# A new step order for a fused attention and MLP kernel, with half of w_out scaled by ScalarE in 128-column steps

## The chip, the cores and the metric

The kernel runs on one core of a Trainium2 chip. A core has five engines with queues of their own: TensorE (PE, matrix products), VectorE (DVE), ScalarE (ACT), GpSimd (POOL) and SyncE (SP, which here only issues DMAs). The metric is device time in microseconds (us), lower is better. All times below come from three runs and one profiled execution of the kernel before.

## The reference, cut to what matters

Two parts, the second fed by the first. In the attention part every 32-element row x of q and k is turned into 64 features, all products of 8 + 8 projections; then kv and the normalisation are sums over 1088 positions, for 4 batches and 4 heads:

```python
phi(x) = outer(S1 @ x, S2 @ x).reshape(64)       # for each row of q and of k
kv  = einsum('bhsf,bhsd->bhfd', phi(k), v);  z = phi(k).sum(over s)
num = einsum('bhsf,bhfd->bhsd', phi(q), kv)
x   = num / (einsum('bhsf,bhf->bhs', phi(q), z)[..., None] + 1e-6)
```

The result, 4352 tokens of 128, goes through an MLP with 2048 hidden units:

```python
h = x @ w_in;  g = h * sigmoid(beta * h);  out = g @ w_out
```

## The kernel before, in words

**The MLP.** Column j of w_in is multiplied by beta (tile `winb`, f16) and row j of w_out by 1/beta (tile `woutp`, f16), so that the activation is a plain SiLU and needs no scale. w_in and w_out come and are scaled in four quarters of 512 columns or rows: steps `wb0` to `wb3` (line 340) and `wo0` to `wo3` (line 343). The tokens go in ten chunks (seven of 512, three of 256). A chunk's 16 blocks of hidden units are taken in "waves" of 1024 f32 PSUM columns, 68 waves in all. Step `f<n>a`/`f<n>b` (line 885) writes the two halves of wave n with x @ winb; with the second half ACT's SiLU (line 894, tile `gT`) is issued. Step `s<n>a`/`s<n>b` (lines 917 and 909) multiplies gT by woutp and adds into the chunk's accumulator. Wave tiles have two PSUM buffers, so PE can be at most two waves ahead of ACT. Quarter 0 of winb and woutp serves waves 0 and 1 of a chunk, quarter 1 waves 2 and 3, and so on. Steps `o<n>` store a chunk: a transpose on DVE, and DMAs on SP's queue.

**The attention,** once for each batch b: load k and q (`lk`, `lq`) and v (`lv`); turn k (`kta`, `ktb`, DVE), project (`kpj`, PE), turn back (`ktn`, DVE, tile `tk`), build the feature products in four pieces (`kp0` to `kp3`, POOL or DVE), and sum them with v on PE (`kv0` to `kv3`, line 610). For q the same (`qt`, `qpj`, `qtn`), with the denominators (`zs` to `dr`), scaled by the inverse (`an`), products (`qp`), turned (`qpt`, DVE). Then `num` (PE, line 708) gives the tokens and `xa`, `xb`, `xc` (ACT or DVE) copy them to `xall`, from which the waves read. Batch 0 goes another way, so that the first wave can start early: its first 512 tokens are done in a part of their own (`qt0x0`, `qpjx0`, `cpjx0`, `dpx0`, `numx0`), the denominators are spread by PE (`rxa0`, `rxb0`, line 564, tile `dr`), copied by ACT (`ry0`, line 574) and multiplied in by DVE (`xm00`, `xm10`, line 579). beta is spread to all partitions by PE for the first two quarters (`bp0`, `bp1`, line 317) and copied by ACT (`by0`, `by1`), and by DMA for the others (`lba2`, `lba3`). Small set-up steps stand first: `ls1`, `ls2`, `sp`, `sp2` for S1 and S2, `lb`, `lbb`, `bt`, `bc`, `rb` for beta.

**Idle matmuls.** A step `i<n>` issues n matmuls of zeros, 128x512 (line 373), whose result nobody reads; they only keep PE at work. Before has 16 of them.

**What sets the order.** There is no scheduler at run time. `ORDER` is a list of step names written out in full; the kernel runs through it and issues each step's instructions, so it fixes every engine's program order and the order of the DMAs on SP's queue. The engines run on their own, tied by semaphores. `ENGINES` says which engine does a step that could run on several ("p" POOL, "v" DVE, "a" ACT). A DMA on SP also waits until the eighth DMA before it has landed.

```python
    for name in ORDER.split():
        if name[0] == "i" and name[1:].isdigit():
            idle(int(name[1:]))
        else:
            ops.pop(name)()
```

## Time and profile before

| | |
|---|---|
| three runs | 103.53, 103.75 and 108.78 us, median 103.75 us |
| profiled execution | 103.81 us, of which the profile's span is 102.1 us |
| busy in the span | PE 96.1, ACT 74.9, DVE 59.8, POOL 50.9 us |
| first wave's first matmul | 19.28 us into the span |
| first SiLU | 19.92 us |
| last matmul's end | 98.5 us |

The table's last three lines are from the timeline of the profile. A busy PE is not PE at its peak: matmuls overlap, and a busy stretch can hold slow matmuls. Lines of the profile name an engine, the source line, the operation and the tiles, "out<-in". In the view of the chain, the work that ended last is followed backwards: each line has a start, a length and what ran then. "x4" counts instructions, "[2.01 <-PE wave L885]" says how long the engine had been idle before and what released it.

### The profile page before, as it was taken

The page shows a single profiled execution, that of the slowest core. Times are in us where ns is not written, and L with a number is a line of the kernel's source. Part 1 is how long each engine was busy: PE and PEld are TensorE (multiplying, and loading weights), DVE is VectorE, ACT ScalarE, POOL GpSimd, SP SyncE. Part 2 cuts the span into 40 slices and gives each one's busy share as a digit, 9 for nine tenths or more (in the row PEclk, how much of TensorE's full clock was granted, in tenths as well). Part 3 has the DMA queues.
Part 4 walks back from the last instruction along what each step waited for, and adds up shares of the span by engine and source line. Part 5 has one row for each costly group of instructions (what it writes and reads, how often), then busy time and mean ns, then how long its engine had stood idle before and what let it go on. Part 6 is the DMA issues. An engine that isn't in the chain of part 4 may idle for free.

```text
span 102.1 us, 3119 instructions
## 1 busy us (share of the span) xinstructions
PE 96.1 (94%) x1308; PEld 49.7 (49%) x1308; DVE 59.8 (59%) x109; ACT 74.9 (73%) x96; POOL 50.9 (50%) x60
## 2 busy tenths in 40 slices
PE   5999998999999999999999999999999999999960
PEld 1353468335444545353445454434444435689950
DVE  1256696799895795589996469698635020111110
ACT  1411526296798597478999669999968999999940
POOL 6503999498799997038997419539300000000000
PEclk9999999999999999999999999999999999999999
DMA  2999995789218628615620050123012214014221
GB/s 40 349 258 334 359 307 172 223 272 290 87 38 288 113 51 234 197 24 87 182 75 13 13 95 5 39 50 53 0 23 37 50 25 77 0 29 78 47 58 51
DMA packets 23998, 12.05 MB, mean 118 GB/s; under 512 B 17008, under 2 KB 21936, under 8 KB 23984
## 3 DMA queue, kind: packets, MB, share of 16 engines
q1 hardware_dynamic: 23744, 11.77, 43.6%
q8 instruction: 10, 0.16, 0.7%
q10 hardware_dynamic: 240, 0.08, 0.3%
q14 instruction: 4, 0.03, 0.2%
HBM read 9.32 MB, written 2.23 MB: 113 GB/s over the span
## 4 chain that ended last, share of the span: by engine, by line
PE 82%; ACT 10%; DVE 3%; issue 1%; ACTq 0%
PE wave L885 27%; PE acc L917 20%; ACT gT L894 9%; PE idle L373 5%; PE xp L708 5%; PE at L610 4%; PE fin L909 4%; PE kpp L390 3%; PE qpp L471 3%; PE kvb L610 1%; PE xw L708 1%; PE bw L317 1%; PE at L491 1%; PE at L434 1%; PE dr L564 1%
## 5 line engine op out<-in xcount | busy, mean ns | idle before, releaser
L894 ACT ACTIVATE gT<-wave 128x1024 f16<-128x1024 f32 (+1 forms) x69 | 65.3, 1017 | 8.0 <-PE wave L885 7.2
L885 PE MATMUL wave<-xall,winb 128*128 128x512 f16 (+1 forms) x128 | 36.2, 366 | 0.3
L917 PE MATMUL acc<-gT,woutp 128*128 128x512 f16 (+1 forms) x128 | 34.4, 365 | 0.0
L885 PEld LDWEIGHTS <-winb 128*128 128x128 f16 x160 | 14.8, 98 | 16.0 <-issue 4.7
L917 PEld LDWEIGHTS <-woutp 128*128 128x128 f16 x128 | 12.4, 97 | 12.8 <-issue 0.6
L405 POOL TENSOR_TENSOR kp<-tk 128x512 f32<-128x512 f32 (+1 forms) x11 | 14.1, 1306 | 5.4 <-DVE tk L401 5.4
L844 DVE STREAM_TRANSPOSE osb<-acc 128x512 f32<-128x512 f32 (+1 forms) x8 | 5.4, 680 | 14.9 <-PE acc L917 11.3
L598 DVE STREAM_TRANSPOSE qpt<-qp 128x768 f32<-128x768 f32 (+1 forms) x13 | 11.3, 890 | 1.0 <-POOL qp L405 0.9
L405 POOL TENSOR_TENSOR qp<-an,tq 128x768 f32<-128x768 f32 (+1 forms) x7 | 10.8, 1557 | 1.7 <-DVE an L546 1.5
L373 PE MATMUL idle<-warm 128*128 128x512 f16 x16 | 6.9, 566 | 1.3 <-DVE tiny L232 1.3
L377 DVE STREAM_TRANSPOSE kT<-k_in 128x576 f32<-128x576 f32 (+1 forms) x8 | 5.7, 717 | 3.3 <-DMA k_in<-in_k_dram 3.3
L708 PE MATMUL xp<-qpt,kvr 32*32 32x288 f32 (+2 forms) x160 | 6.9, 364 | 0.0
L708 PE MATMUL xw<-qpt,kvr 32*32 32x256 f32 (+1 forms) x160 | 6.9, 343 | 0.0
L523 POOL TENSOR_TENSOR prod<-tq,tcc 128x288 f32<-128x288 f32 (+1 forms) x4 | 3.3, 814 | 7.1 <-DVE tq L483 5.6
L650 POOL TENSOR_TENSOR bz<-tq,zw 128x768 f32<-128x768 f32 x2 | 4.3, 2180 | 3.8 <-ACT zw L644 3.8
L382 DVE STREAM_TRANSPOSE qT<-q_in 128x512 f32<-128x512 f32 (+1 forms) x8 | 5.6, 700 | 0.0
L340 POOL TENSOR_TENSOR winb<-w_in_sb,beta_all 128x512 f16<-128x512 f32 x4 | 5.4, 1352 | 0.4 <-DMA w_in_sb<-in_moe_w_in_dram 0.4
L610 PEld LDWEIGHTS at<-kp,v_in 128*32 128x32 f32 (+1 forms) x216 | 3.5, 109 | 3.0 <-issue 1.7
L708 PEld LDWEIGHTS xp<-qpt,kvr 32*32 32x32 f32 x160 | 3.7, 103 | 2.5 <-DVE kT L377 0.5
L885 PE MATMUL wave<-xlast,winb 128*128 128x256 f16 x32 | 4.8, 271 | 0.0
L610 PE MATMUL at<-kp,v_in 128*32 128x64 f32 (+1 forms) x216 | 4.8, 223 | 0.0
L405 DVE TENSOR_TENSOR qp<-an,tq 128x768 f32<-128x768 f32 x4 | 4.8, 1194 | 0.0
(106 smaller groups left out, 97.9 us busy)
## 6 DMA issues: line engine op xcount, KB each, us to landing
k_in<-in_k_dram SPq DMA_DIRECT2D x6, 272.0 KB, 4.2
q_in<-in_q_dram SPq DMA_DIRECT2D x6, 272.0 KB, 6.3
v_in<-in_v_dram SPq DMA_DIRECT2D x8, 144.0 KB, 4.1
v_in<-in_v_dram SPq DMA_DIRECT2D x8, 128.0 KB, 2.9
w_in_sb<-in_moe_w_in_dram SPq DMA_DIRECT2D x4, 256.0 KB, 4.7
w_out_sb<-in_moe_w_out_dram SPq DMA_DIRECT2D x4, 256.0 KB, 4.3
out_dram<-osb SPq DMA_DIRECT2D x16, 64.0 KB, 1.9
beta_all<-in_moe_beta_dram SPq DMA_DIRECT2D x2, 256.0 KB
```

The costliest lines, as they stand in the source:

```text
L340: eng(name).tensor_tensor(out=winb[:, s], in0=w_in_sb[:, s], in1=beta_all[:, s], op=ALU.mult)
L373: nc.tensor.matmul(out=t[:, 0, :], lhsT=warm[:, 0:P], rhs=warm, start=True, stop=True)
L377: nc.vector.transpose(out=kT[:, u0:u1, :].rearrange("p u t -> p (u t)"), in_=k_in[b][:, u0 * D : u1 * D])
L382: nc.vector.transpose(out=qT[:, u0:u1, :].rearrange("p u t -> p (u t)"), in_=q_in[b][:, u0 * D : u1 * D])
L405: eng.tensor_tensor(out=ap(o, g0 * F, [[F, n], [R, R], [1, R]]), in0=ap(a, g0 * a_step + a_off, [[a_step, n], [1, R], [0, R]]), in1=ap(bsr ...
L598: nc.vector.transpose(out=ap(st[b]["qpt"], c0 * H * F, [[1, (c1 - c0) * H * F]]), in_=ap(st[b]["qp"], c0 * H * F, [[1, (c1 - c0) * H * F]]),)
L610: nc.tensor.matmul(out=t[T * h : T * h + T, :], lhsT=v_in[b][:n, h, c, :], rhs=kp[:n, 4 * c + h, :], start=(done == 0), stop=(done == NC - 1),
L708: nc.tensor.matmul(out=ts[j][T * h : T * h + T, 0 : n * T], lhsT=st[b]["kvr"][p : p + T, f, h, :], rhs=ap(st[b]["qpt"], (4 * c0 + h) * F + ...
L844: nc.vector.transpose(out=osb[:, :un, :].rearrange("p u m -> p (u m)"), in_=accs[ci][:, : un * T])
L885: nc.tensor.matmul(out=wvs[s][:, w, i * n : i * n + n], lhsT=winb[:, j * P : j * P + P], rhs=xlast[:, u0 * T - LAST0 :][:, :n] if ci in tu ...
L894: nc.scalar.activation(out=g[:, o + i * 512 : o + i * 512 + 1024 // m], in_=wvs[s].rearrange("p a n -> p (a n)")[:, i * 512 : i * 512 + 10 ...
L917: nc.tensor.matmul(out=accs[ci][:, :n], lhsT=woutp[:, j, :], rhs=gts[s // GP][:, o : o + n], start=(j == 0), stop=(j == NJ - 1),)
```

## The change

Two things change at once. The scaling of w_out gets a second way: a quarter whose name is not in `ENGINES` is done by ACT, in four activations of 128 columns with the scale in a per-partition operand, in place of one POOL multiplication of 512 columns. That holds for quarters 0 and 1 (`wo0`, `wo1`); quarters 2 and 3 stay on POOL.

```diff
     def w_out_scale(name, i):
+        if name not in ENGINES:
+            for j in range(4 * i, 4 * i + 4):
+                scaled(woutp[:, j, :], w_out_sb[:, j, :], rbeta[:, j : j + 1])
+            return
         eng(name).tensor_tensor(
```

`scaled` is `nc.scalar.activation(out=out_, in_=in_, func=ACTF.Copy, scale=scale)` (line 277).

And both lists, `ORDER` and `ENGINES`, are written anew from end to end; they hold the same steps apart from the idle ones. Only stretches of `ORDER` are shown, cut at their ends. Up to the first wave:

```diff
-    ls2 lk0b warm lk0a i2 ident lq0a masks ls1 i5 sp lb sel pads tbl kta0 lbb i2 zms sbd i1 sp2 ktb0 bt kpj0
-    lq0b s2s qt0x0 ktn0 kp30 lv01 lv00 bc i2 rb zs0 qt00 lv03 zc0 qpjx0 lv02 bp0 ty0 qtnx0 wp0 wm0 li0 i1 by0
-    cpjx0 kp00 ctnx0 i3 lk11 bp1 lo1 tz0 kp20 dpx0 kp10 lk10 dsx0 qp10 drx0 qp00 qpt00 qpt10 lo0 li2 kv20 kv30
-    kv10 by1 kv00 kvw0 rz0 lba2 li1 wb0 kvt0 rxa0 lq10 kvc0 lq11 rxb0 wo1 numx0 kta1 lo3 wo0 ry0 cpj0 ktb1 xm00
-    xm10 lk20 qpj0 f0a wb2 f0b
+    masks ident ls1 warm lk0b lk0a i4 lq0a lq0b ls2 lv00 lv01 i3 lv03 sp i3 lv02 lb lq10 pads sel tbl lo2 ktb0
+    zms lk11 sbd lk10 kta0 kpj0 lbb sp2 li0 lo1 lo0 li1 qt0x0 bt lq11 s2s bc i3 ktn0 kp30 qt00 qpjx0 zs0 i2 ty0
+    zc0 qtnx0 kp00 tz0 wp0 rb wm0 bp1 cpjx0 kp10 ctnx0 bp0 by0 qp10 dpx0 dsx0 lba2 by1 kp20 drx0 qp00 kv30 kv00
+    lo3 kv20 qpt10 kv10 kvw0 kvt0 wo2 rz0 wb0 i2 qpt00 li2 rxa0 rxb0 kvc0 kta1 ktb1 numx0 ry0 wo1 cpj0 xm00 qpj0
+    xm10 li3 f0a ctn0 lba3 qtn0 lk20 wo0 f0b
```

After the first wave the steps of batches 1 to 3 keep their rough places among the waves. Around the four `num` steps, and at the end:

```diff
-    s3b wm1 f6a qpt20 f6b cpj1 num0 wo2 xa0 f7a xb0 lv10 xc0 f7b s4a
+    s3a s3b s4a wm1 kp11 qpt20 s4b ktb2 f7a kp01 f7b cpj1 num0 ctn1 s5a
...
-    s11a qpt11 f14a s11b qpt01 kr11 kp22 kr31 f14b s12a s12b lv20 s13a s13b lv22 f15a qpt21 f15b qt12 num1
+    qpt21 s10b kr31 s11a f14a f14b wp2 s11b s12a s12b f15a lk30 qpt01 kr11 s13a f15b kta3 num1
...
-    kp03 s23b f27a f27b kv23 f28a su03 f28b o2 kv33 num2 xa2 xc2 xb2 su13 kv03 su23
+    s21a s21b s22a f26a f26b s22b f27a kr12 f27b lv33 kv13 kp33 kr32 su13 kv33 su03 num2 xb2 xa2 kv23 su23
...
-    s39b f45a f45b num3 xa3 f46a
+    s39b qpt23 num3 o4 f46a xa3 f46b
...
-    s63a s63b o7 o8 f67a f67b s64a s64b s65a s65b s66a s66b s67a s67b o9
+    s63a s63b f67a f67b s64a s64b s65a s65b s66a s66b s67a s67b o8 o9
```

In `ENGINES` these change hands. From POOL to DVE: `wb3 dp0 an1 dp2 an2 kp23 su13 su23`. From DVE to POOL: `qp20 kp21 kp31 su33 su43`. From ACT to DVE: `xb1 xc2 zy3`. From DVE to ACT: `xb2 zc2`. From POOL to ACT: `wo0 wo1`. Of the batch 3 steps `bz` and `qp` one each is on DVE and two on POOL, before as after. There are 17 idle matmuls where there were 16; the last two stand between `kvt0` and `rxa0`.

## The prediction

> **What bounds the kernel now.** I read the page's busy times, then the chain of work that ended last, then PE's timeline in the first 14 us, ACT's timeline round the first SiLU, and the windows of 5 us.

> ```profile
> PE 96.1 (94%) x1308; PEld 49.7 (49%) x1308; DVE 59.8 (59%) x109; ACT 74.9 (73%) x96; POOL 50.9 (50%) x60
> ...
> PE 82%; ACT 10%; DVE 3%; issue 1%; ACTq 0%
> ```

> PE carries 82% of the chain, ACT 10%. The chain up to the first wave:

> ```profile
> 7.16 1.23 PE kpp L390 x16
> ...
> 8.41 0.78 DVE tk L401
> ...
> 13.71 1.46 PE kvb L610 x72
> ...
> 15.61 0.71 PE kvb L685 x4
> 16.32 0.96 PE dr L564 x8
> ...
> 18.84 0.51 PE qpp L471 x16
> ```

> PE waits little, but is slow at first:

> ```profile
> 1.25 3.17 PE L373 MATMUL idle<-warm 128*128 128x512 f16 x7 [1.25 <-DVE tiny L232]
> 4.51 0.30 PE L283 MATMUL cb<-ident,s 16*32 16x16 f32 x8
> 4.74 1.46 PE L373 MATMUL idle<-warm 128*128 128x512 f16 x3
> 6.13 0.63 PE L297 MATMUL cb<-s,sel 16*128 16x32 f32 x2
> 8.23 1.04 PE L373 MATMUL idle<-warm 128*128 128x512 f16 x2
> 12.24 0.82 PE L373 MATMUL idle<-warm 128*128 128x512 f16 x3
> ```

> The idle matmuls follow each other every 0.43 us up to 9 us and every 0.22 us at 12.24. The trace's record of the granted clock (1.0) begins at 10.49 us; before it PE runs at half pace. And the steady part:

> ```profile
> 40.00:45.00 5.00, 5.00 (x118) 2.47 (x118) 3.36 (x7) 3.09 (x5) 0.97 (x2) 1.00 0.48 141
> 65.00:70.00 5.00, 4.91 (x23) 2.00 (x21) 4.32 (x7) 5.00 (x6) 2.42 (x3) 1.00 0.32 58
> 80.00:85.00 5.00, 4.92 (x23) 2.13 (x22) 0.72 (x1) 4.93 (x6) 0.00 (x0) 1.00 0.23 40
> ```

> At 40 us PE is full and ACT has 1.9 us free; from 65 us both are full. PE's own work from the first wave (19.28 us) to the last matmul (98.5) sums to 76.4 us: 512-column matmuls at 0.216, `num` 1.5, `kpj` and `qpj` 0.65, a batch's `kv` 1.4. It took 79.2, so 2.8 us are stalls, 1.2 of them between `num2` and `num3`, where ACT is full. So the time is: first wave (19.28), plus 76.4, plus stalls (2.8), plus the end (3.6 to the span's 102.1), plus 1.7 outside the span.

> **The change, part by part.**

> *Start, order of steps.* Before, after the last idle matmul of the second group PE does `sp2` and `bt` (6.13 to 7.09) and only then `kpj0`. After, `kpj0` comes right behind three idles and `sp2`, `bt` follow it, under DVE's `tk`. kT is no hindrance: `ktb0` and `kta0` with `sbd` between end near 5.8 (k landed at 3.6 and 4.5, transposes 0.7 each). So `kpj0` starts at 6.13, 0.96 earlier, and `tk` ends 0.96 earlier, at 8.2.

> *Start, pace of PE.* The switch came 3.40 us after `kpj0` began, the first stretch that streams nearly without a hole. I cut the time back from it in like lengths and count streaming by idles at 0.43 and `kpj0` by its groups: 0.25 to 3.66, 71%; 3.66 to 7.08, 54% and some tiny matmuls; 7.08 to 10.49, 70 to 89%, depending on how the 0.65 us of `zs0` count. Only the last released the clock. After, 3.66 to 7.08 holds 0.56 + 1.28 of idles and 0.95 of `kpj0`: 82%. That lies nearer the stretch that sufficed, so I take the release at 7.08; the other end is 10.49, as before.

> [...]

> With the release at 7.08: `sp2`, `bt` to 7.7; three idles 0.65 to 8.35; `qpjx0` 0.3 and `zs0` 0.55 to 9.2; `zc0` (ACT 0.17) while two idles run; `wp0` 9.85; `wz` 10.45; `bp1`, `cpjx0`, `bp0` (0.6, 0.33, 0.57) to 11.6. Then `kv`, before at 13.63. Its inputs: `kp30`, `kp20` on POOL 8.2 + 2.53 = 10.75, `kp10` on DVE 11.1, v landed 9.55. Gain 2.0. Behind `kv` everything is as before but for the two idles between `kvt0` and `rxa0`: +0.43. Net −1.6 at the first wave, 17.7. With the release at 10.49 the same sum gives `kv` at 12.9 and the first wave at 18.95: −0.3.

> *DMAs in the start.* On SP one half of q1, quarter 2 of w_out and k1 go ahead of quarter 0 of w_in. Loads landed at some 0.65 us for 272 KB and v ended at 9.55, so quarter 0 lands near 12.8, quarter 1 near 14.6 and the last near 18. The first wave needs `wb0` (1.27, done 14.2): hidden, with 3 us to spare. k2 waits for `kta1`, `ktb1`, but the weights now stand ahead of it: nothing.

> *w_out on ACT.* Eight activations of 128x128 sit behind `drs`:

> ```profile
> 7.25 0.82 ACT L277 ACTIVATE s2sel<-cb,zmask 128x32 f32<-128x32 f32 x4 [3.62 <-PE cb L306]
> 17.32 0.59 ACT L574 COPY drs<-dr 128x512 f32<-128x512 f32 x1 [0.59 <-PE dr L564]
> 19.92 3.77 ACT L894 ACTIVATE gT<-wave 128x1024 f16<-128x1024 f32 x4 [2.01 <-PE wave L885]
> 28.14 0.43 ACT L725 CAST xall<-xw 128x128 f16<-128x128 f32 x2 [0.71 <-PE xw L708]
> ```

> The same helper starts one every 0.17 us for 32 columns, the casts of 128 take 0.27 and start 0.16 apart. Bounds 8 x 0.16 = 1.3 and 8 x 0.27 = 2.2; I take 1.6. ACT was idle for 2.01 there, so the first SiLU is late by 0 to 0.2, and ACT has slack until 55 us: 0. POOL loses two steps of 1.04, off the path: 0. Without the idle 2.01 the 1.6 would go straight onto the first SiLU.

> *Steady part.* PE has the same instructions: 0. ACT gives up three copies (`xb1` 0.37, `xc2` 0.65, `zy3` 0.37) and gets two (0.37, 0.2): −0.8, of which only `xc2`, `zy3` and `xb2` lie in the stretch where ACT is full: −0.6, or nothing where PE is the later. DVE, busy for 32.6 of the 40 us from 20 to 60, gets 1.6 more: in come `wb3` 0.65, `dp0` 0.3, `an1`, `an2`, `dp2` 0.46 each, `kp23`, `su13`, `su23` 0.65 each, `xb1` 0.42, `xc2` 0.75, `zy3` 0.4; out go `qp20` 1.2, `kp31` 0.99, `kp21` 0.65, `su33`, `su43`, `xb2` 0.4 each, `zc2` 0.17. So the feature products must be checked where PE asks for them, in us from the first wave. `num1`: `cpj1` ends at 8.2, `tcc` 8.9, `dp1` on POOL (1.15) 10.0, `den` and `rden` (0.49, 0.38) 10.9; `an1`, now on DVE, stands behind `o0` (its chunk ends near 11.2) and a transpose, 0.72 each, and ends at 13.2; POOL's three `qp` (1.48 each, 31.23 to 35.68 before) at 17.7, the last `qpt` at 19.0; PE arrives at 19.5. `num2` needs `qpt` at 32.2 to 33; PE arrives at 34.4. `zm3` needs POOL's `su43` at 37; PE arrives at 37.8. On SP, `kr11` is issued behind k3's half near 16.4 and lands in 1.9, before `num1`; `lv33` near 29.5 and lands in 2.9, before `kv13` at 33.6. All in time, margins 0.5 to 1.5. `o8` now stands behind the last `s`, but on DVE and SP its place is the same: 0. Stalls as before: 0, bounds −1 and +2 (three POOL products at the 1.7 that contended rows show, thrice).

> Sum: 103.8 − 1.6 = 102.2 us. The profiled execution (103.81) stands 0.06 over the median of the runs.

> **Rivals.**
> 1. *Clock released at 10.49 as before.* For it: 3.66 to 7.08 has two holes, and the busy columns of the windows do not tell the stretches apart (3.34 us each in 3.66:7.08 and 7.08:10.49). Against: 82%. Time: 103.8 − 0.3 = 103.5.
> 2. *Clock released later, at 13.9; ends slower.* After, 7.08 to 10.49 holds `sp2` and `bt`, tiny matmuls of 0.9 us, so if 82% was too little this stretch, some 75%, is too. Then the idles, `bp1` and `bp0` run at half pace (+0.43, +0.4, +0.4), `kv` starts at 14.2, the first wave 1.0 later: 104.8. It decides where a stretch must fill over about 82%.
> 3. *DVE becomes the bound.* If `an1`, `qp`, `qpt` come over 0.5 us late at `num1`, PE waits there, and likewise at `num2` and `zm3`. Price 0.7 a place, 2 in all, on the 103.5 of rival 1: 105.5. Against: DVE's share of 59%.

> [...]

> **How the numbers follow.** Forecast 45% (102.2; its own range 101.2 to 103.2, from the steady part's −1 and the SiLU's delay), rival 1 25%, rival 2 12%, rival 3 13%, and 5% for the forecast with fewer stalls still (101). The range 101.0 to 105.3 leaves out some 2 in 10. A measurement of this kernel can tell about 2% (2.1 us) from no change. Faster by that (under 101.7): a third of the forecast and the 5%, 0.20. Slower (over 105.8): the worse halves of rivals 2 and 3, 0.13. Same: 0.67.

> **What would show it.** `kpj0` at 6.1 and `tk` ending near 8.2; the idles ahead of `qpjx0` at 0.22 apart (forecast) or 0.43 (rivals); `kv` at 11.6, 12.9 or 14.2; the first wave at 17.7, 18.95 or 20.3; eight ACT rows of some 0.2 ahead of the first SiLU without a gap over 0.3; last matmul 79 us after the first wave. I am wrong if PE waits over 1 us at `num1`, `num2` or `zm3`, or if the w_out rows cost over 0.3 each.

## The result, and the profile after

| | before | after |
|---|---|---|
| median of six runs each | 103.38 us | 109.62 us |
| ratio, 95% interval | | 1.056, 1.048 to 1.065 |
| profiled execution, its span | 103.81, 102.1 us | 108.83, 107.1 us |
| first wave's first matmul | 19.28 us | 23.27 us |
| first SiLU | 19.92 us | 24.14 us |
| last matmul's end | 98.5 us | 103.5 us |
| from first wave to last matmul | 79.2 us | 80.2 us |

The change makes the kernel 5.6% slower; 102.2 us was forecast, 101.0 to 105.3 as the range. Of the 5.0 us between the two profiled executions, 4.0 are there when the first wave starts, and 1.0 is added behind it. Medians are over all executions; the ratios here and below leave out those more than 1.5% above the fastest of the same kernel. The page of after, its busy times, the clock in 40 slices (2.7 us each) and the shares of the chain:

```profile
PE 99.0 (92%) x1309; PEld 52.6 (49%) x1309; DVE 61.1 (57%) x113; ACT 76.1 (71%) x103; POOL 45.7 (43%) x55
...
PEclk9999555699999999999999999999999999999997
...
PE 65%; ACT 16%; DMA 8%; POOL 2%; SPq 2%; issue 2%; DVE 1%; POOLq 0%
```

PE is busy for 2.9 us more with one more instruction, and the clock is full, then half for some ten us, then full again. DMAs, absent from the chain of before, hold 8% of it. The chain of after, in order of time:

```profile
3.67 5.08 DMA beta_rows<-in_moe_beta_dram
9.18 0.75 PE idle L376 x3
...
15.20 2.44 PE kvb L613 x72
18.09 1.22 PE kvb L688 x4
...
20.16 1.13 PE dr L567 x8
21.90 2.34 ACT woutp L276 x8
24.24 0.91 ACT gT L897
...
40.81 3.73 DMA kvr<-kvr
```

The chain begins at the load of beta, 16 KB in two DMAs on ACT's queue, issued at 3.67 us and landed at 8.75. Before, beta was no part of the chain. `kv` takes 2.44 us where it took 1.46. After it come the w_out steps on ACT, 2.34 us, and, some 17 us later, a small copy on SP's queue that takes 3.73. PE's timeline of after in the start (line numbers are three higher or one lower than before):

```profile
4.59 1.46 PE L376 MATMUL idle<-warm 128*128 128x512 f16 x3
5.98 1.11 PE L393 MATMUL kpp<-kT,sbd 64*32 64x288 f32 x16
7.01 0.40 PE L296 MATMUL cb<-s,sel 16*128 16x32 f32 x2
8.79 0.39 PE L305 MATMUL cb<-ident,beta_rows 16*128 16x16 f32 x2 [1.37 <-DMA beta_rows<-in_moe_beta_dram]
9.11 0.82 PE L376 MATMUL idle<-warm 128*128 128x512 f16 x3
...
11.03 1.03 PE L376 MATMUL idle<-warm 128*128 128x512 f16 x2
...
15.13 2.46 PE L613 MATMUL kvb<-kp,v_in 128*32 128x64 f32 x72
```

The reader should see three things. `kpj0` starts at 5.98, as forecast (6.1). `bt` (line 305) waits 1.37 us for beta. And the three idles at 9.11 take 0.82, as at full clock, while the two at 11.03 take 1.03, as in the slow start of before (two in 1.04 at 8.23): PE had the full clock and lost it. The windows of 3.41 us show that, cut where the record of the granted clock changes; behind each stretch stand PE's busy time and, third from the end, the clock:

```profile
6.85:10.26 3.41, 2.04 (x34) 0.99 (x26) 1.44 (x2) 0.99 (x6) 2.18 (x2) 1.00 1.01 264
10.26:13.68 3.42, 3.42 (x64) 2.63 (x56) 1.97 (x5) 0.61 (x3) 2.41 (x3) 0.50 0.86 267
13.68:17.09 3.41, 3.41 (x80) 2.55 (x76) 2.84 (x8) 1.07 (x2) 1.18 (x1) 0.50 1.01 304
17.09:20.50 3.41, 2.92 (x29) 2.25 (x22) 1.23 (x2) 1.26 (x3) 2.11 (x3) 0.50 1.05 364
```

The clock came at 6.85, where the forecast had it at 7.08. In the stretch that followed PE worked for only 2.04 us, because of the wait at `bt`; at its end the clock went back to half, for three stretches (10.24 us), until 20.5.

Why beta is late shows on POOL and on ACT's queue. First before, then after:

```profile
0.80 0.20 POOL L238 MEMSET beta_rows<- 128x128 f32 x1 [0.29 <-POOLq L952]
```

```profile
1.77 0.34 ACTq L204 DMA_DIRECT2D beta_rows<-in_moe_beta_dram  x1
```

```profile
0.80 0.10 POOL L244 MEMSET hmask<- 128x4 f32 x1 [0.29 <-POOLq L955]
0.95 0.47 POOL L246 MEMSET hmask<- 32x1 f32 x4
1.52 0.19 POOL L247 TENSOR_TENSOR pmask<-hmask 128x2 f32<-128x2 f32 x1
1.65 0.21 POOL L237 MEMSET beta_rows<- 128x128 f32 x1
```

```profile
3.67 0.34 ACTq L203 DMA_DIRECT2D beta_rows<-in_moe_beta_dram  x1
```

The instructions of that line hold one more, a wait on ACT's queue that ends at 3.6:

```profile
L203 ACTq EVENT_SEMAPHORE  x1: 17/17/17, 3.6 to 3.6; - x1
```

The new order begins with `masks ident` where before had `ident` ahead of `masks`. Both are POOL's, and `ident` also clears `beta_rows`, the tile that the load fills. So the clearing ends at 1.86 in place of 1.00. The load does not follow at 1.9, though, but at 3.67. The operands in the trace say what ACT's queue waits for: semaphore 102, which the first half of k raises as it lands, sixteen times from 3.10 to 3.59 (DVE's turn of it starts at 3.61). Beta's load raises the same semaphore next. In the trace of after the 103 DMAs of SP and ACT raise eight semaphores between them, each 12 or 13 times, and 88 of the 95 that raise one again start eight places behind the DMA that raised it before, the others seven, nine or ten. Each of the 95, and of before's 95 as well, starts 16 ns or more behind the last raise on record of that earlier DMA. Between that half of k and the load stand the other half, two loads of q, two of S and three of v. In before, beta's load has a semaphore, 106, that no DMA had used, goes out at 1.77 and waits for the clearing alone; there the loads of v come behind it, at 2.67 to 4.74, and wait in its place. How a load comes by its semaphore when the program is built is not shown; it is not by the place in the list alone, as x1 and x4 below show. From issue to landing the load takes 5.1 us; in before, beta's two loads took 2.9 and 3.2.

### The profile page after: what moved, and what is told of

It reads as the page before. It is cut to its first block, busy times and chain, and to the rows that moved or that the text cites. A ratio compares the mean times of both kernels' runs of the same rounds, so it can differ in the third digit from the quotient of the medians.

```text
span 107.1 us, 3122 instructions
## 1 busy us (share of the span) xinstructions
PE 99.0 (92%) x1309; PEld 52.6 (49%) x1309; DVE 61.1 (57%) x113; ACT 76.1 (71%) x103; POOL 45.7 (43%) x55
## 2 busy tenths in 40 slices
DMA packets 23998, 12.05 MB, mean 113 GB/s; under 512 B 17008, under 2 KB 21936, under 8 KB 23984
## 4 chain that ended last, share of the span: by engine, by line
PE 65%; ACT 16%; DMA 8%; POOL 2%; SPq 2%; issue 2%; DVE 1%; POOLq 0%
PE wave L888 20%; PE acc L920 16%; ACT gT L897 13%; DMA beta_rows<-in_moe_beta_dram 5%; PE at L613 4%; PE xp L711 4%; DMA kvr<-kvr 3%; PE fin L912 3%; PE idle L376 2%; PE kvb L613 2%; ACT woutp L276 2%; PE qpp L474 2%; PE bw L316 2%; PE kpp L393 1%; PE at L494 1%
## 5 line engine op out<-in xcount | busy, mean ns | idle before, releaser
L920 PE MATMUL acc<-gT,woutp 128*128 128x512 f16 (+1 forms) x128 | 34.9, 366 | 0.0
L920 PEld LDWEIGHTS <-woutp 128*128 128x128 f16 x128 | 12.4, 99 | 12.9 <-issue 1.5
L408 POOL TENSOR_TENSOR kp<-tk 128x512 f32<-128x512 f32 (+1 forms) x12 | 14.8, 1260 | 4.6 <-DVE tk L404 4.6
L408 POOL TENSOR_TENSOR qp<-an,tq 128x768 f32<-128x768 f32 (+1 forms) x8 | 13.4, 1698 | 7.7 <-DVE an L549 7.7
L601 DVE STREAM_TRANSPOSE qpt<-qp 128x768 f32<-128x768 f32 (+1 forms) x13 | 11.2, 890 | 0.9 <-POOL qp L408 0.9
L376 PE MATMUL idle<-warm 128*128 128x512 f16 x17 | 7.5, 585 | 1.3 <-DVE tiny L231 1.3
L711 PE MATMUL xp<-qpt,kvr 32*32 32x288 f32 (+2 forms) x160 | 7.6, 364 | 0.4 <-DMA kvr<-kvr 0.4
L380 DVE STREAM_TRANSPOSE kT<-k_in 128x512 f32<-128x512 f32 (+1 forms) x8 | 5.7, 720 | 3.9 <-DMA k_in<-in_k_dram 3.9
L339 POOL TENSOR_TENSOR winb<-w_in_sb,beta_all 128x512 f16<-128x512 f32 x3 | 3.8, 1272 | 3.5 <-ACT beta_all L325 2.9
L486 DVE STREAM_TRANSPOSE tq<-qpp 128x576 f32<-128x576 f32 (+2 forms) x5 | 3.3, 663 | 3.5 <-PE qpp L474 3.4
L912 PE MATMUL fin<-woutp,gT 128*128 128x128 f16 x64 | 4.4, 219 | 0.0
```

Source lines behind the costliest of these rows:

```text
L376: nc.tensor.matmul(out=t[:, 0, :], lhsT=warm[:, 0:P], rhs=warm, start=True, stop=True)
L380: nc.vector.transpose(out=kT[:, u0:u1, :].rearrange("p u t -> p (u t)"), in_=k_in[b][:, u0 * D : u1 * D])
L408: eng.tensor_tensor(out=ap(o, g0 * F, [[F, n], [R, R], [1, R]]), in0=ap(a, g0 * a_step + a_off, [[a_step, n], [1, R], [0, R]]), in1=ap(bsr ...
L601: nc.vector.transpose(out=ap(st[b]["qpt"], c0 * H * F, [[1, (c1 - c0) * H * F]]), in_=ap(st[b]["qp"], c0 * H * F, [[1, (c1 - c0) * H * F]]),)
L711: nc.tensor.matmul(out=ts[j][T * h : T * h + T, 0 : n * T], lhsT=st[b]["kvr"][p : p + T, f, h, :], rhs=ap(st[b]["qpt"], (4 * c0 + h) * F + ...
L912: nc.tensor.matmul(out=accs[ci][a][:, 0:DM], lhsT=gts[s // GP][:, o + a * P : o + a * P + P], rhs=woutp[:, j, :], start=(j == 0), stop=(j ...
```

## The experiments

In all of them the theory is: **masks ahead of ident makes beta late; PE's hole at `bt` costs the clock; the clock costs the 4 us at the first wave.** The rivals: the hole's own time; the ACT steps for w_out; some other part of the new order. Each ratio is against the kernel before, measured with it on the same chip. f0 is the first wave's first matmul; "none" stands where too few executions were left for a ratio.

| kernel | median us | ratio, 95% interval | `bt` at | half pace again | `kv` at | f0 | f0 to last matmul |
|---|---|---|---|---|---|---|---|
| before | 103.38 | 1 | 6.58 | no | 13.63 | 19.28 | 79.2 |
| after | 109.62 | 1.056, 1.048 to 1.065 | 8.79 | 10.26 to 20.50 | 15.13 | 23.27 | 80.2 |
| y1 after, ident first | 102.53 | 0.995, 0.988 to 1.002 | 7.33 | no | 11.62 | 17.61 | 80.2 |
| y2 before, masks first | 111.17 | 1.069, 1.054 to 1.083 | 9.59 | 8.39 to 25.45 | 18.86 | 27.00 | 79.5 |
| z1 after, `bt` later | 103.42 | 1.010, 1.006 to 1.015 | 8.63 | no | 11.62 | 17.63 | 80.6 |
| z4 after, hole filled | 105.07 | 1.028, 1.022 to 1.034 | 9.14 | no | 13.45 | 19.45 | 80.1 |
| x1 after, load listed early | 108.59 | 1.048, 1.037 to 1.059 | 8.78 | 10.87 to 21.11 | 14.84 | 23.40 | 80.4 |
| x2 after, three idles moved | 107.68 | none | 9.88 | 12.53 to 22.77 | 15.40 | 24.36 | 79.7 |
| x3 after, w_out on POOL | 109.73 | none | 8.88 | 7.98 to 21.64 | 16.30 | 24.42 | 80.4 |
| y3 y1, w_out on POOL | 103.00 | 1.000, 0.995 to 1.005 | 6.63 | no | 11.56 | 17.57 | 80.3 |
| y4 before, w_out on ACT | 104.01 | 1.004, 0.998 to 1.010 | 6.40 | no | 12.31 | 17.95 | 79.8 |
| x4 before, load listed late | 102.89 | 0.998, 0.992 to 1.004 | 6.34 | no | 12.25 | 17.89 | 79.6 |
| z2 y1, `kr11` earlier | 102.31 | 0.993, 0.988 to 0.998 | 6.62 | no | 10.95 | 16.96 | 79.9 |
| z3 z2, two idles less | 101.78 | 0.992, 0.988 to 0.996 | 6.87 | no | 12.05 | 17.69 | 79.3 |

The columns behind the ratio are of one profiled execution each. They move by up to some 1.4 us with the place where the clock first comes (x4, in nearly before's order, has it at 6.26 and f0 at 17.89, before at 10.49 and 19.28); in these executions that place lay anywhere from 4.04 to 10.49 us.

### First look: beta, the hole, and w_out

*x1_beta_early.* The steps that load beta go to the front of the list.

```diff
-    masks ident ls1 warm lk0b lk0a i4 lq0a lq0b ls2 lv00 ... lv02 lb lq10 ... kpj0 lbb sp2
+    masks ident ls1 ls2 lb lbb warm lk0b lk0a i4 lq0a lq0b lv00 ... lv02 lq10 ... kpj0 sp2
```

> The changed kernel with one thing moved back: the two small loads of beta's rows (lb, lbb, and ls2 ahead of them) stand right behind ls1, ahead of k, q and v. Theory H (the late beta leaves PE without work from 7.4 to 8.8 us, that hole costs the clock from 10.3 to 20.5 us): beta lands before 5 us, no wait ahead of line 305, the clock stays full from about 6.9 us on, first wave at 17.7 to 18.3 in place of 23.27, time 103.0 to 104.3. Rival W (the eight ACT steps of w_out ahead of the first SiLU are the cost): the first wave moves by 1.4 us at most, time 107 or more. Rival S (the order behind the first wave is the cost): time 106 or more.

The edit missed its aim: the load still went out only at 3.54 us and landed at 8.7, where after has 3.67 and 8.75; by estimate from after's trace it waited for k's first half there too. So 108.59 says nothing of an early beta. It does say that the place in the list does not decide when this load goes.

*x2_idle_over_beta.* The three idle matmuls behind `bt` go ahead of it.

```diff
-    li1 qt0x0 bt lq11 s2s bc i3 ktn0
+    li1 qt0x0 i3 bt lq11 s2s bc ktn0
```

> The changed kernel with beta's rows as late as they are, but the three idle matmuls that stood behind bt now ahead of it, so that PE is busy while beta is awaited. Theory H: the clock stays full after 10.3 us although beta still lands at 8.7, first wave at 18.3 to 19.3, time 103.8 to 105.3. If the lateness of the data itself is the cost and not the clock: first wave at 22 or later, time 107.5 or more. Rivals W and S: no change from 108.8 by more than 1.

PE had the clock at 5.70 in this execution, so the idles were over at 7.7, and beta landed only at 9.9. From PE's timeline of x2:

```profile
6.86 0.82 PE L376 MATMUL idle<-warm 128*128 128x512 f16 x3
9.88 0.39 PE L305 MATMUL cb<-ident,beta_rows 16*128 16x16 f32 x2 [2.20 <-DMA beta_rows<-in_moe_beta_dram]
```

Three idles were too few: the hole is 2.20 us, longer than in after, and the clock went again. Of the four executions one had a granted clock of 0.999 over its span and took 103.58 us; the three others had 0.95 to 0.96 and took 106.9 to 109.4. The same kernel goes either way.

*x3_wout_pool.* `"wo1": "p", "wo0": "p"` are put back into `ENGINES`; the order is that of after.

> The changed kernel with both ACT quarters of w_out given back to POOL, at the same places of the order. Rival W: 2 us and more are gained, 106.8 or less. Theory H: the ACT steps ended 0.25 us after the first wave was ready, so 0 to 0.5 is gained, 108.3 to 109.2, and the clock is lost from 10.3 to 20.5 as before.

109.73 us, half a us over what the theory gave and 2.9 over the most that rival W allows: the ACT steps are not what makes after slow.

*x4_before_beta_late.* In before, the second half of q0 and the loads of v are listed ahead of beta's load.

```diff
-    ls1 i5 sp lb sel
+    ls1 lq0b lv01 lv00 lv03 lv02 i5 sp lb sel
```

> The kernel before with the loads of v and the second part of q0 put ahead of beta's rows, all else the same: beta's load then waits for the DMA eight places before it. Theory H: beta lands near 9 us, PE waits at line 306 for about 2 us, and the clock comes later than 10.49 us or goes again; first wave 2 to 4 us later, time 105 to 107.5. Rivals W and S: 103.2 to 104, as this kernel has neither the ACT steps nor the new order.

Again the list did not decide: the load went at 1.75, `bt` had no wait at 6.34, and nothing changed (0.998). The run is not a test of a late beta. What it does show is the spread of the start: its first wave came 1.4 us ahead of before's with the clock there at 6.26 and not at 10.49.

### One exchange, both ways

*y1_ident_first* is after with its first two steps exchanged, and *y2_before_masks_first* is before with the same two steps exchanged the other way.

```diff
-    masks ident ls1 warm lk0b lk0a i4
+    ident masks ls1 warm lk0b lk0a i4
...
-    ls2 lk0b warm lk0a i2 ident lq0a masks ls1 i5
+    ls2 lk0b warm lk0a i2 masks ident lq0a ls1 i5
```

> The changed kernel with two words of the order swapped: ident ahead of masks. POOL then clears beta's rows first, beta's load is numbered among the first eight DMAs and waits for no other. The run with lb moved did not test theory H: beta's load still went out at 3.54 us and landed near 8.7. Theory H, now tested: the load goes out near 1.8 us and lands by 5.5, no wait ahead of line 305, PE has no hole between 7 and 9 us, the clock once granted stays, first wave at 17.5 to 18.6, time 102.5 to 104.5. Rival C (the small f32 matmuls of the start lose the clock by themselves, hole or no hole): the clock goes between 7 and 14 us all the same, first wave past 21, time 106.5 or more. Rivals W and S: 106 or more with the clock kept.

> The kernel before with the same two words swapped the other way: masks ahead of ident, nothing else. Theory H: beta's load goes out near 3.6 us in place of 1.8 and lands near 8.7; line 306 stands ahead of kpj0 here, so kpj0 waits until 9.2 in place of 7.1, the clock comes later or goes again, first wave at 21.5 to 25, time 105.5 to 109.5. If H is wrong and something else of the new order is the cost: 102.5 to 104.

This exchange alone takes after from 1.056 of before to 0.995 (109.62 to 102.53 us), and before itself to 1.069 (111.17). The timelines of PE, y1 first:

```profile
6.12 1.04 PE L393 MATMUL kpp<-kT,sbd 64*32 64x288 f32 x16
7.09 0.40 PE L296 MATMUL cb<-s,sel 16*128 16x32 f32 x2
7.33 0.37 PE L305 MATMUL cb<-ident,beta_rows 16*128 16x16 f32 x2
...
11.62 1.48 PE L613 MATMUL kvb<-kp,v_in 128*32 128x64 f32 x72
```

```profile
9.59 0.60 PE L306 MATMUL cb<-ident,beta_rows 16*128 16x16 f32 x2 [3.67 <-DMA beta_rows<-in_moe_beta_dram]
10.12 1.21 PE L390 MATMUL kpp<-kT,sbd 64*32 64x288 f32 x16
...
18.86 2.46 PE L610 MATMUL kvb<-kp,v_in 128*32 128x64 f32 x72
```

In y1 `bt` follows without a wait, and `kv` starts at 11.62, to the digit where the forecast had it. In y2 the hole is 3.67 us, since `bt` stands ahead of `kpj0` there, and the half pace lasts five stretches, to 25.45. That is more than the theory gave (105.5 to 109.5, the first wave at 21.5 to 25; measured 111.17 and 27.00), so its size was missed, not its direction. So this part of the new order carries the loss whichever list it stands in. It does not yet tell the hole's own time from the clock, or a late beta from a late PE.

### The hole without the wait, the wait without the hole

*z1_bt_later* leaves beta as late as in after but asks for it later; *z4_idle_eight* asks as early as after but fills the hole.

```diff
-    qt0x0 bt lq11 s2s bc i3 ktn0 kp30 qt00 qpjx0 zs0 i2
+    qt0x0 lq11 s2s i3 ktn0 kp30 qt00 qpjx0 zs0 bt bc i2
...
-    li1 qt0x0 bt lq11
+    li1 qt0x0 i8 bt lq11
```

> The kernel after, with `bt` and `bc` moved behind `zs0`; masks still ahead of ident, so beta's load is as late as in after (issued at 3.7, landed at 8.7), but PE asks for it only near 9. Theory (PE's hole of 1.4 us at `bt` costs the clock of the next three stretches): no hole of over 0.5 us between 6 and 10 us, the clock stays at 1.0 once it has been granted, kv at 11.6, first wave at 17.7, 102.5 to 103.3 in all, like the kernel with ident first. Rival A (the clock goes for another reason that the new order brings, masks first being only its companion): half pace from 10 on as in after, first wave past 22, 107 to 109. Rival B (the late load itself costs, by what else reads beta): the clock is kept, but `bp1` or `by1` waits, first wave near 19.

> The kernel after, with eight idle matmuls more just ahead of `bt`: beta as late as in after, the same 1.4 us filled with work that nobody needs. Theory (the hole costs the clock): the clock is kept, PE reaches the later steps 1.7 us later than with ident first, first wave at 19.0 to 19.4, 104.0 to 104.8. Rival (the wait's own time is the loss, not the clock): nothing gained, 108 to 109. With eight idles at half pace (3.4 us), if the clock is not there yet, first wave 21 and 106.

PE's timelines, z1 first, then z4:

```profile
6.96 0.82 PE L376 MATMUL idle<-warm 128*128 128x512 f16 x3
7.71 0.45 PE L474 MATMUL qpp<-qT,sbd 64*32 64x128 f32 x16
8.09 0.61 PE L437 MATMUL cb<-tk 128*32 128x16 f32 x36
8.63 0.39 PE L305 MATMUL cb<-ident,beta_rows 16*128 16x16 f32 x2
...
11.62 1.48 PE L613 MATMUL kvb<-kp,v_in 128*32 128x64 f32 x72
```

```profile
7.00 1.90 PE L376 MATMUL idle<-warm 128*128 128x512 f16 x8
9.14 0.39 PE L305 MATMUL cb<-ident,beta_rows 16*128 16x16 f32 x2 [0.24 <-DMA beta_rows<-in_moe_beta_dram]
...
11.80 0.71 PE L316 MATMUL bw<-beta_rows,ident 32*128 32x128 f32 x8
```

z1 has masks first and beta issued at 3.64, and yet `kv` starts at 11.62 and all four executions take 103.2 to 103.5 with a mean clock of 0.998 or more, where the six of after had 0.93 to 0.95: without the hole the clock stays, in the profiled one from 5.91 to the last matmul. z4 separates the clock from the wait's own time. It makes PE work through just the time that after spends waiting, 1.73 us of matmuls that nobody reads, starts `bt` 0.35 us later than after did, and comes to 1.028 of before where after has 1.056. Its clock stays at 1.0 from 6.06 on. So the time alone is not the loss. Nor is it nothing: of the 5.9 us between the spans of y1 and after (101.2 and 107.1), 2.0 are still there in z4 (103.2), 1.8 of them at the first wave, and 3.9 are gone with the loss of the clock. By the ratios (0.995, 1.028 and 1.056) the two parts are 3.3 and 2.8%, so their sizes are known only to an us or so; that both are there is clear of the noise.

Both came out a little above what was expected, z1 by 0.1 over its range and z4 by 0.3 over its. z1 also stands 1.0% above before (1.006 to 1.015) where y1 does not, though its first wave comes at the same time as y1's; in the profiles 0.4 us lies between the first wave and the last matmul (80.6 and 80.2), and what the late load still costs there was not traced.

### w_out on ACT alone, and on POOL with the fault taken out

*y3_ident_first_wout_pool* is y1 with `wo0`, `wo1` back on POOL. *y4_before_wout_act* is before with the part that the change is named for: `wo1 wo0` behind `ry0`, on ACT in steps of 128.

```diff
-    kvc0 lq11 rxb0 wo1 numx0 kta1 lo3 wo0 ry0 cpj0
+    kvc0 lq11 rxb0 numx0 kta1 lo3 ry0 wo1 wo0 cpj0
```

> The first of these four, with both ACT quarters of w_out given back to POOL as well. With the clock kept the first SiLU comes after the eight ACT steps of 0.29 each; without them it should start when its wave is ready. Theory H: 0.2 to 0.6 us less than the first of these four, or no difference that can be told. Rival W: 2 us less.

> The kernel before with the named part of the change alone: quarters 0 and 1 of w_out on ACT in steps of 128 columns, put right behind ry0, where the changed kernel has them; the order is otherwise that of before. Eight starts 0.29 apart after drs (17.9 us) end near 20.3, 0.35 after the first wave is ready (19.92). Theory H: 103.3 to 104.3, no difference that can be told from before. Rival W: 105.5 or more.

Neither makes a difference that can be measured: y4 is at 1.004 (0.998 to 1.010), and y3 at 1.000 where y1 is at 0.995, with intervals that overlap. ACT's timeline of y4:

```profile
16.00 0.59 ACT L578 COPY drs<-dr 128x512 f32<-128x512 f32 x1 [0.59 <-PE dr L568]
16.48 2.45 ACT L277 ACTIVATE woutp<-w_out_sb,rbeta 128x128 f16<-128x128 f32 x8
18.83 1.91 ACT L898 ACTIVATE gT<-wave 128x1024 f16<-128x1024 f32 x2
```

The eight steps take 2.45 us, one every 0.29; the prediction had taken 1.6, one every 0.20. They use up the 2.01 us that ACT had free, and the first SiLU starts 0.88 us behind the first wave in place of 0.64: 0.24 late, once.

### The 1.0 us behind the first wave

PE's timeline of after at `num1`:

```profile
43.57 0.67 PE L711 MATMUL xp<-qpt,kvr 32*32 32x288 f32 x2
44.59 0.42 PE L711 MATMUL xp<-qpt,kvr 32*32 32x288 f32 x1 [0.36 <-DMA kvr<-kvr]
...
46.14 0.69 PE L494 MATMUL at<-qT,wz 128*32 128x288 f32 x8
```

`num1` takes 2.57 us here. It stalls behind its first rows for `kr11`, the last of three small DMAs on SP that spread kv (`kr21`, `kr31`, `kr11`). It is issued behind k3's half (`lk30`) and lands 3.73 us after its issue. *z2_ident_first_kr_first* puts `kr11` ahead of `lk30` in y1, and *z3_no_late_idle* also leaves out the two idles ahead of `rxa0`.

```diff
-    s12b f15a lk30 qpt01 kr11 s13a
+    s12b f15a kr11 lk30 qpt01 s13a
...
-    wo2 rz0 wb0 i2 qpt00 li2 rxa0
+    wo2 rz0 wb0 qpt00 li2 rxa0
```

> The kernel after with ident ahead of masks, and `kr11` ahead of `lk30` on SP's queue. Theory (of the 1.0 us that the part behind the first wave has become longer, most is `kr11`'s small copy, which lands 3.6 us after its issue because it stands behind k3's half): it lands in 1.9 to 2.2, `num1` is no longer held up, last matmul 79.4 to 79.6 us behind the first wave in place of 80.2, 101.7 to 102.0 where ident first alone gave 102.5. Rival (PE is late there for its own sum of work and DVE's products): 80.2 as before, 102.5.

> As the kernel with ident and `kr11` first, and the two idle matmuls between `kvt0` and `rxa0` left out (15 idles in all). PE went from `kvt0` over the idles straight into `rxa0`, whose input (`rz0`) had been ready when the idles began: first wave 0.4 earlier, 17.2, and 101.3 to 101.6. Rival (the copy `kvr` or the w_out quarter decides): the same time as with the idles, 101.7 to 102.0. If a stretch with a hole of 0.3 us lost the clock, 106.

From SP's timeline of z2, and then from its timeline of waves:

```profile
33.55 1.88 SPq L678 DMA_DIRECT2D kvr<-kvr  x3
35.48 0.59 SPq L179 DMA_DIRECT2D k_in<-in_k_dram  x1
```

```profile
20.77 1.26 POOL L339 TENSOR_TENSOR winb<-w_in_sb,beta_all 128x512 f16<-128x512 f32 x1 [0.36 <-DMA w_in_sb<-in_moe_w_in_dram]
...
22.09 0.60 PE L888 MATMUL wave<-xall,winb 128*128 128x512 f16 x2 [0.80 <-POOL winb L339]
```

The small copies now go together. The last of them still takes 3.0 us to land, more than the 1.9 to 2.2 expected, but it is there before PE comes to `num1`, and `num1` takes 1.50 us (38.23 to 39.73): the 1.07 us that it took longer in after account for the 1.0 behind the first wave. But z2 as a whole only comes to 102.31 against y1's 102.53. In the profiled execution its first wave was there at 16.96, and then wave 4 waited 0.80 for quarter 2 of w_in, which landed near 20.6 and is scaled on POOL: part of an early start is given back there. z3, whose first wave came at 17.69, shows no such wait at that wave and needs 79.3 us to the last matmul, what before needs. That the late copy held up `num1` is shown; the expected time was 0.3 too low for z2 and 0.2 for z3. In z3 `num` of the first tokens comes 3.58 us behind `kv` and not 3.94 as in z2 and y1, so the two idles did cost 0.36.

z3 is the fastest measured, 0.992 of before (0.988 to 0.996): the new order with ident first, `kr11` first and 15 idles. It gains 0.4 to 1.2%. Its interval overlaps those of z2 and y1, so that it beats these is not shown.

## Why the prediction was wrong

*The step that failed* is "`sp2`, `bt` to 7.7". It took beta to be there, as before, and put no price on the wait of `bt`. The working traced SP's queue past the moves, but not POOL's first steps nor ACT's queue: `masks` ahead of `ident` moved the clearing of `beta_rows` by 0.85 us, beta's load came behind three loads of v and had to wait for the semaphore of k's first half, raised last at 3.59, and it landed at 8.75. `bt` waited 1.37. y1, with the two steps exchanged, has no such wait, and `kv` at 11.62.

*What the step then decided* is the clock, and it was only thought of in one direction. The prediction weighed when the clock would come (7.08, 10.49 or 13.9) and held it for certain from then on. It came at 6.85, before the hole, and was taken away behind it. The forecast's sum to the first wave was 17.7; after had 23.27, 5.6 later: `kv` started 3.5 later (15.13 against 11.6), and from `kv` to the first wave it took 8.1 where 6.1 was summed, at half pace.

*The steady part* was taken at 0 and cost 1.0. Its upper bound used POOL products of 1.7, which before's trace has (three `kp` of 128x768, 1.715 in the mean); that they were contended no run shows. The term that was off is "`kr11` ... lands in 1.9": it landed in 3.73 behind k3's half, 21.3 us after the first wave, when PE had come to it at 20.3. With 5.6 at the start this is the whole miss of 6.6 in the profiled execution (102.2 to 108.83).

*w_out on ACT*: 1.6 was taken, with 1.3 and 2.2 as bounds; it is 2.45 in y4, outside. The price at the end is small all the same (0.24), since only what exceeds ACT's 2.01 idle counts, as the text said. The nearest row had been that of casts without a scale operand, 0.27 long and 0.16 apart. In after the eight steps are 0.387 to 0.404 long and start 0.292 to 0.304 apart.

*The quarters of w_in* were put at 14.6 for quarter 1 and "near 18" for the last. Quarter 2, the third of the four, landed only at 20.6 in z2 and 21.2 in z1. In after that was hidden by the late first wave; in z2 and z1 it holds wave 4 by 0.7 to 0.8.

*What held*: `kpj0` at 6.1 (5.98), `kT` no hindrance, the clock near 7.08 (6.85), and, with the fault taken out, `kv` at 11.6 (11.62 in y1) and the first wave at 17.7 (17.61).

*What was luck*: the gain of 1.6 us that these numbers stood for is mostly not the order's. The profiled execution of before had its clock only at 10.49; in the 13 other profiles it came between 4.04 and 6.86. Two of these, x4 and y4, start in nearly before's order, with `bt` ahead of `kpj0`: clock at 6.26 and 6.38, first wave at 17.89 and 17.95, only 0.3 behind y1's. So an early clock does not need the fuller stretch of the new order, and y1 as a whole cannot be told from before (0.995, 0.988 to 1.002). That its median of 102.5 lies near the 102.2 of the forecast says little about the forecast's working.

No rival was right. Rival 2 has half pace in the start, but by a late release; rival 3, DVE as the bound, shows nowhere. The prediction's own sign of being wrong, over 1 us lost at `num1`, did show (1.07), but for the copy of kv: the products were ready, the copy was not.

## What to carry to other kernels

When a list is reordered, follow every queue from its first instruction, the small ones too: a memset that moved by 0.85 us moved the issue of a 16 KB load by 1.9 and its landing by some 4, because it then shared its semaphore with a load of k that landed at 3.59. Ask of each wait in the start not only how long it is but whether the tensor engine stands still in it; here a wait was better put behind work (z1, 1.010) or filled with it (z4, 1.028) than left where a few small matmuls depended on it (after, 1.056). And see what is in flight ahead of a load or a small copy: from issue to landing it took 2.9 us in before and 5.1 in after for beta, 1.9 in before and 3.7 in after for the last of kv's rows. One profile of a kernel's start is one draw: the clock came at 10.49 us in before and at 4.04 to 6.86 in the 13 others, so see where it came in others before a gain is put down to the order.

## What the runs showed of the hardware

*A hole of 1.37 us in a stretch of 3.41 took the clock of after.* Between two changes in the record of the granted clock lie whole multiples of 3.413 us (1 to 5, 25, 27 and 28 of them). PE's idle time (above 0.12 us at once) in the stretches ahead of the loss, against those that kept it:

| kernel | stretch at full clock | idle in it | clock after it |
|---|---|---|---|
| y2 | 4.97 to 8.39 | 2.48 | half, five stretches |
| after | 6.85 to 10.26 | 1.37 | half, three |
| x1 | 4.04 to 7.46, then 7.46 to 10.87 | 1.17, then 1.32 | full, then half, three |
| x3 | 4.57 to 7.98 | 1.52 | half, four |
| x2 | 5.70 to 9.11, then 9.11 to 12.53 | 1.43, then 1.42 | full, then half, three |
| z3, y3, x4, y4 | first at full clock | 0.5 to 0.8 | full |

*Busy at half pace did not bring it back.* From 10.26 to 17.09 PE of after is busy without a break (3.42 of 3.42 and 3.41 of 3.41 us above), mostly with small f32 matmuls, and the clock stayed at half through both stretches; in y2 it took five. Two stretches that are full in the record did not release the clock here. What would have was not tried.
